# Chunks 2 to 5 of a Mamba-2 scan done as units of 64 tokens, in a fused scan and feed-forward kernel

## The chip, the cores and the metric

One core of a Trainium2 chip runs the whole program. Its engines work in parallel and meet through semaphores: TensorE (matmuls; PE in the profile, with its weight loads as PEld), VectorE (DVE), ScalarE (ACT), GpSimd (POOL) and SyncE (SP), which here issues nearly all DMAs. The metric is the device time of the program in microseconds; less is better.

## The reference

Two layers, one after the other, all in float32. The first is a state-space scan over 4 sequences of 768 tokens with 8 heads, head size 32 and state size 16, cut into chunks. In one chunk, with `cum` the running sum of log `a`:

```python
L = np.exp(cum[:, :, :, None] - cum[:, :, None, :]) * causal
M = np.einsum('bhin,bhjn->bhij', Cc, Bc) * L
y_intra = np.einsum('bhij,bhjd->bhid', M, xc)
y_inter = np.einsum('bhin,bhnd->bhid', Cc, state) * np.exp(cum)[:, :, :, None]
y[:, :, sl] = y_intra + y_inter
Bx = np.einsum('bhjn,bhjd->bhjnd', Bc, xc) * np.exp(cum[:, :, -1:] - cum)[:, :, :, None, None]
state = np.exp(np.sum(la, axis=-1))[:, :, None, None] * state + np.sum(Bx, axis=2)
```

The result doesn't depend on the length of a chunk, only the split of the work between `y_intra` and `y_inter` does. The second layer takes the 3072 rows of 256 values (8 heads of 32):

```python
h = x @ w_in            # 256 -> 2048
g = h * np.cos(h)
out = g @ w_out         # 2048 -> 256
```

## The kernel before

The kernel splits each sequence into 6 chunks (`NC`) of 128 tokens. For each chunk, all 4 sequences give 512 rows for the second layer, which is done in 16 visits (`NF`), 96 in all. A visit `n` with `c, f = divmod(n, 16)` takes half of the rows of chunk `c` and 256 of the 2048 columns: `first(n)` multiplies by `w_in` (line 726), `wind` and `gate` form the cosine (ACT lines 733 and 748, DVE line 739), `gated` multiplies (DVE line 753), `differ` forms three differences on POOL (lines 778 to 781) and `second(n - 2)`, for chunk 1 onward `seven` (line 835), multiplies by `w_out` two visits later (`LAG`). `seven` multiplies 128-column pieces in seven products.

Each engine runs its instructions in the order of the code; there is no scheduler that reorders. Tiles come from pools: a name (tag) has a number of buffers, and the first instruction that writes a new tile waits until the last user of the tile that had the buffer is done. This holds for DMAs too: SP then stands at the DMA, and those behind it in its queue stand as well. The results of `first` have two buffers in PSUM (tag `h`), the products of the scan two pairs of banks (`pair`).

The scan is done between the visits, a chunk ahead of them. Chunks 0 and 1 are done as four units `k` = 0 to 3 of 64 tokens (`W`): `decays0` scans the decays of 64 tokens for all 8 heads and 4 sequences, with the two sequence pairs on the two halves of the partitions; `inner` (line 481) forms C·B, `weights` (DVE line 490) multiplies it with the decays, and `finish0` adds to one result the part of the old state (line 506), the sums for the new state (line 515) and the part of the unit's own tokens (line 523). `weigh0` (POOL line 406) scales B for the sums, in the buffer `sc0`. The times at which units 2 and 3 do this are in `unit_at`: unit 3's `finish0` is at the end of visit 21. `add` in it forms the state after unit 3 on POOL in visit 22, and four DMAs (line 558) move half of it to the partitions where chunk 2 looks for it.

Chunks 2 to 5 are done as 128 tokens of two pairs of sequences `u`. Per chunk: `decays` (line 583, 8 scans), `weigh` (line 566), `reaches` (line 574), `turn_blocks` (transposes on DVE, line 597, of blocks of B and C that `load_blocks` fetched), `turn2` (ACT line 607), `intra2` (line 624), `masked` (line 645, which multiplies only the blocks on and under the diagonal), and after visit 14 of the chunk before, `open2` (lines 656 and 664), `finish2` (line 676) and `carry` (lines 698 and 702), which forms the new state. `plan`, `halves_of` and `block_loads` say in which visits; DVE work that is not a visit's own stands in the list `behind`, one item of it ahead of `gated` and the rest after it.

In the printout that follows, the line numbers are the profile's.

Of the kernel before, what the change touches and what calls it, by code (L numbers as in the profile page):

```python
# [25 lines left out]
def kernel(  # L26
# [31 lines left out]
    rows = ctx.enter_context(tc.tile_pool(name="rows", bufs=NB))  # L58
    scan = ctx.enter_context(tc.tile_pool(name="scan", bufs=2))
    states = ctx.enter_context(tc.tile_pool(name="states", bufs=3))  # L60
# [16 lines left out]
    raw, arow, along, blocks = {}, {}, {}, {}  # L77
# [15 lines left out]
    def load(c, seqs=(0, NB), only=(B, C, x)):  # L93

        if not 1 < c < NC:
            return
        if c not in raw:
            raw[c] = (loads.tile([P, 2, NB * H, N], FP32, tag="bc", name="bc"),
                      loads.tile([P, NB, H, D], FP32, tag="xr", name="xr"))
        bc, xr = raw[c]  # L100
        xr = xr.rearrange("p b h d -> p (b h) d")
        for dst, src in ((bc[:, 0], B), (xr, x)):

            if not any(src is o for o in only):
                continue
            for b in range(*seqs):
                rs = slice(b * H, (b + 1) * H)
                for t in range(2 if b % 2 else 1):
                    n = W if b % 2 else P
                    ts = slice((n - t * W) % P, (n - t * W) % P + n)  # L110
                    nc.sync.dma_start(
                        out=dst[ts, rs], in_=src[b:b + 1, :, c * P + t * W:c * P + t * W + n, :]
                        .rearrange("b h s n -> s (b h) n"))

# [4 lines left out]
    bs, cs = ([t[:, i].rearrange("p (k q h) n -> p k q (h n)", k=2, q=2)[:, k]  # L119
               for t in both for k in range(2)] for i in range(2))  # L120
# [3 lines left out]
    def load_b(k, s, eng=nc.sync, of=B):  # L124

        eng.dma_start(out=(bs if of is B else cs)[k][s * W:(s + 1) * W].rearrange(
# [18 lines left out]
    def group(q, b):  # L145
        return slice(32 * (q ^ b % 2), 32 * (q ^ b % 2) + 32)

    def load_blocks(c, u):
# [3 lines left out]

        blocks[c, u] = to_ = loads.tile([P, 2, 2, 2, 4 * N], FP32, tag="blocks", name="blocks")
        for s in range(2):
            for k, src in enumerate((B, C)):
                of = src[2 * u + s, :, c * P:(c + 1) * P].rearrange(
                    "(q h) (t m) n -> h q t (m n)", h=2, m=4)
                if s == 0:
                    for h in range(2):
# [1021 lines left out]
```

## Time and profile before

| | |
|---|---|
| median of 3 runs | 369.29 us (369.17 to 369.72) |
| the profiled execution | 369.34 us, its span 367.5 us |
| mean granted TensorE clock | 0.998 |
| TensorE busy | 361.1 us (98%) |
| DVE, POOL, ACT busy | 275.3, 217.8, 172.9 us |
| `first` (line 726) | 768 instructions, 183.3 us busy |
| `seven` (line 835) | 1106 instructions, 174.9 us busy in four groups |
| scan matmuls of chunks 2 to 5 (lines 624, 656, 664, 676) | 256, 128, 96, 256 instructions |
| DMA | 30.57 MB, 97706 packets |

A float32 matmul of the code is two instructions in the profile. Small matmuls run beside each other in parts of the array, so their mean durations overlap and don't add up: what a group takes is read from its start to the start of the group behind it, in the timeline. The first line of a group in the timeline holds the start, the time to the end of its last instruction, the engine, the source line, the tiles (output<-inputs), the shape and the number of instructions.

### The profile page before, as it was taken

To read this page: it belongs to the slowest core of one execution; us is meant where nothing else is said; L and a number is where in the kernel's file an instruction comes from. 1 tells how busy PE (TensorE), PEld (TensorE's weight loads), DVE (VectorE), ACT (ScalarE), POOL (GpSimd) and SP (SyncE) were. 2 spreads that over 40 slices of the span, in tenths; PEclk is the share of its full clock that TensorE was granted. 3 is DMA by queue.
4 is the path that set the end of the run, shared out by engine and by line. 5 is a ranking of instruction groups with operands and counts; after the bars stand their busy time and mean duration, and the time that the engine had idled before them with its cause. 6 is when DMAs were issued, how large, how long until landed. Compare 5 with 4: busy or idle time off the path is not lost.

```text
span 367.5 us, 8762 instructions
## 1 busy us (share of the span) xinstructions
PE 361.1 (98%) x3390; PEld 324.9 (88%) x3390; DVE 275.3 (75%) x452; ACT 172.9 (47%) x300; POOL 217.8 (59%) x340
## 2 busy tenths in 40 slices
PE   7999999999999999999999999999999999999995
PEld 4788888899999899999899999989999989999995
DVE  7789998568699857888867987777887783544463
ACT  4588766453445244444344344434444534443432
POOL 6567666679786568765346674544584444554441
PEclk9999999999999999999999999999999999999999
DMA  7996947366226646731054341020100010010011
GB/s 138 264 365 134 213 108 117 47 172 177 62 74 92 137 110 93 219 86 28 18 78 103 97 128 43 0 54 2 28 14 2 0 30 2 2 29 2 0 30 30
DMA packets 97706, 30.57 MB, mean 83 GB/s; under 512 B 71456, under 2 KB 93568, under 8 KB 97664
## 3 DMA queue, kind: packets, MB, share of 16 engines
q1 hardware_dynamic: 96416, 29.61, 35.3%
q8 instruction: 27, 0.44, 0.5%
q10 hardware_dynamic: 1248, 0.39, 0.5%
q14 instruction: 15, 0.12, 0.1%
HBM read 26.58 MB, written 3.34 MB: 81 GB/s over the span
## 4 chain that ended last, share of the span: by engine, by line
PE 91%; DVE 3%; ACT 2%; issue 1%; DMA 1%; SPq 0%; ACTq 0%; DVEq 0%
PE hp L726 44%; PE o L835 34%; PE o L797 6%; PE y L676 2%; PE g L624 2%; DMA bc<-in_B_dram 1%; DVE mag L281 1%; DVE mag L283 1%; PE g L481 1%; PE y L656 1%; PE y L506 1%; PE y L523 1%; DVE w L739 1%; PE o L880 1%; ACT mag L268 0%
## 5 line engine op out<-in xcount | busy, mean ns | idle before, releaser
L726 PE MATMUL hp<-yT,w_in 128*128 128x256 f32 x768 | 183.3, 382 | 0.5 <-DVE gT L753 0.3
L726 PEld LDWEIGHTS hp<-yT,w_in 128*128 128x128 f32 x768 | 139.4, 190 | 19.9 <-issue 3.2
L778 POOL TENSOR_TENSOR gd<-gT 128x256 f32<-128x256 f32 x79 | 60.0, 760 | 97.0 <-DVE gT L753 84.9
L748 ACT ACTIVATE w<-w,quarter 128x512 f32<-128x512 f32 x96 | 69.2, 721 | 83.8 <-DVE w L739 83.7
L739 DVE SCALAR_TENSOR_TENSOR w<-hp,k 128x512 f32<-128x512 f32 x96 | 65.7, 685 | 44.1 <-ACT k L733 43.9
L733 ACT ACTIVATE k<-hp 128x512 int32<-128x512 f32 x96 | 57.0, 594 | 79.7 <-PE hp L726 79.2
L753 DVE TENSOR_TENSOR gT<-hp,w 128x512 f32<-128x512 f32 x96 | 65.3, 680 | 33.2 <-ACT w L748 21.7
L835 PE MATMUL o<-words,gd 128*128 128x128 f32 x474 | 65.9, 275 | 0.0
L835 PEld LDWEIGHTS o<-words,gd 128*128 128x128 f32 x474 | 59.3, 192 | 0.0
L835 PEld LDWEIGHTS o<-w_out,gT 128*128 128x128 f32 x316 | 47.5, 191 | 4.0
L781 POOL TENSOR_TENSOR gd<-gT,gd 128x128 f32<-128x128 f32 x79 | 45.9, 582 | 6.2
L835 PE MATMUL o<-w_out,gT 128*128 128x128 f32 x316 | 48.0, 274 | 0.0
L780 POOL TENSOR_TENSOR gd<-gT,gd 128x128 f32<-128x128 f32 x79 | 44.0, 557 | 6.2
L583 DVE TENSOR_TENSOR_SCAN lam<-arow,unit 128x512 f32<-128x512 f32 x32 | 42.1, 1314 | 0.0
L835 PE MATMUL o<-words,gT 128*128 128x128 f32 x158 | 30.5, 275 | 0.0
L835 PE MATMUL o<-w_out,gd 128*128 128x128 f32 x158 | 30.5, 275 | 0.0
L797 PE MATMUL o<-w_out,gT 128*128 128x256 f32 x128 | 29.9, 379 | 0.0
L797 PEld LDWEIGHTS o<-w_out,gT 128*128 128x128 f32 x128 | 24.2, 190 | 3.3
L645 DVE TENSOR_TENSOR m<-g,lam 128x256 f32<-128x256 f32 x64 | 24.7, 414 | 0.4
L835 PEld LDWEIGHTS o<-words,gT 128*128 128x128 f32 x158 | 24.0, 192 | 0.0
L835 PEld LDWEIGHTS o<-w_out,gd 128*128 128x128 f32 x158 | 24.0, 192 | 0.0
L852 DVE TENSOR_TENSOR sum<-ps,sum 128x256 f32<-128x256 f32 (+1 forms) x27 | 16.6, 639 | 0.6
(113 smaller groups left out, 280.1 us busy)
## 6 DMA issues: line engine op xcount, KB each, us to landing
arow<-a_cut SPq DMA_DIRECT2D x16, 512.0 KB
words<-in_moe_w_in_dram SPq DMA_DIRECT2D x8, 512.0 KB
words<-in_moe_w_out_dram SPq DMA_DIRECT2D x8, 512.0 KB
out_dram<-sum SPq DMA_DIRECT2D x18, 128.0 KB
xr<-in_x_dram SPq DMA_DIRECT2D x16, 128.0 KB
bc<-in_B_dram SPq DMA_DIRECT2D x16, 64.0 KB
xr<-in_x_dram SPq DMA_DIRECT2D x16, 64.0 KB
arow<-a_cut SPq DMA_DIRECT2D x2, 256.0 KB
```

What stands on the lines that cost most here:

```text
L583: V.tensor_tensor_scan(out=lam[c, b][:, hs].rearrange("p h i -> p (h i)"), data0=rows_.rearrange("p h i -> p (h i)"), data1=unit[:, b % 2 ...
L645: V.tensor_tensor(out=m_[js, :, :, is_], in0=g_[js, :, :, is_], in1=l_[js, :, :, is_], op=ALU.mult)
L726: PE.matmul(to_[:, e], lhsT=w_in[:, k, fs], rhs=y[:, k], start=(k == 0), stop=(k == KT - 1), skip_group_check=True)
L733: ACT.activation(k, hp[n], AF.Copy, bias=0.25, scale=INV_2PI)
L739: V.scalar_tensor_tensor(out=w, in0=hp[n], scalar=INV_2PI, in1=k, op0=ALU.mult, op1=ALU.subtract)
L748: ACT.activation(cos, cos, AF.Sin, bias=quarter, scale=TWO_PI)
L753: V.tensor_tensor(out=gT[n], in0=hp.pop(n), in1=cos, op=ALU.mult)
L778: G.tensor_tensor(out=d[:, 0:2], in0=g[:, 1:2].to_broadcast([P, 2, P]), in1=g[:, 3::-3], op=ALU.subtract)
L780: G.tensor_tensor(out=d[:, 2], in0=g[:, 0], in1=d[:, 0], op=ALU.subtract)
L781: G.tensor_tensor(out=d[:, 3], in0=g[:, 2], in1=d[:, 2], op=ALU.subtract)
L797: PE.matmul(o[c, u][:, t], lhsT=g[:, 2 * e + t], rhs=w_out[:, 2 * j + e], start=(j == e == t == 0), stop=(j == NJ - 1 and e == 1), skip_gr ...
L835: PE.matmul(at[q], lhsT=a_[q], rhs=w[q], start=(j == 0 and q in starts), stop=(j == NJ - 1), skip_group_check=True)
```

## The change

Chunks 2 to 5 are done as two units of 64 tokens each, 2c and 2c + 1, as chunks 0 and 1 are; the two units of a chunk share the visits of the second layer (a visit takes one unit of all four sequences where it took a pair of sequences of the whole chunk), the transposes (`turn_blocks`, `turn2`) and the loads. `intra2` and `masked` become `inner2` and `weights`; `decays` and `weigh` become `decays0` and `weigh0`. The sums of a unit's states are formed one chunk ahead: `finish0(3)` also forms those of units 4 and 5, and `open2(c)` those of chunk c + 1; `take_sums` (ACT) copies them out and `add_state` (DVE) adds the decayed state before. `open2` stays behind visit 14, `finish2` moves behind `first` of visit 15, in front of that visit's `wind`. `steps` says in which visits of the chunk before each part is done; loads of chunk 3 start in other visits than before. Left out below are what is removed with the 128-token form (`load_a`, `decays`, `weigh`, `intra2`, `masked`, `carry`, `plan`, `pairs`, `ends`, the wide `unit`), more buffers (2 for `turned` and `cT2`, 2 for `state`), the layouts of `load_b` and of the output's rows, and the loads of chunk 2, whose rows now come in visits 12 and 13, x in 14 and `along` in 15 and 16.

```diff
-    rows = ctx.enter_context(tc.tile_pool(name="rows", bufs=NB))
+    rows = ctx.enter_context(tc.tile_pool(name="rows", bufs=3))
...
+    def load(c):
+        if c < NC:
+            for k in (2 * c, 2 * c + 1):
+                for s in range(2):
+                    load_b(k, s)
+            for k in (2 * c, 2 * c + 1):
+                for s in range(2):
+                    load_x(k, s)
...
+            blocks[c, s] = to_ = loads.tile([P, 2, 2, 2, 4 * N], FP32, tag="blocks", name="blocks")
+            for p in range(2):
+                for k, src in enumerate((B, C)):
...
+                    if s == 0:
+                        for h in range(2):
+                            nc.sync.dma_start(out=to_[:, k, h, p], in_=of[h])
                         yield
...
+                    for q in range(4 if s else 0):
+                        nc.sync.dma_start(out=to_[group(q, s), k, :, p],
+                                          in_=of[:, q].rearrange("h t f -> t h f"))
+                        if q % 2:
+                            yield
...
         for b in seqs:
-            for q in range(4 if b % 2 else 1):
...
+            s = b // 2
+            for q in range(4 if s else 1):
...
     def weigh0(k):
-        scs[k] = sc = scan.tile([P, 2 * H, N], FP32, tag="sc0", bufs=1, name="sc0")
+        scs[k] = sc = scan.tile([P, 2 * H, N], FP32, tag="sc0", bufs=2, name="sc0")
...
+    def sums(k, at, strip, start=False):
...
+        for p in range(2):
+            for s in range(2):
+                ss = slice(s * W, (s + 1) * W)
+                for q in range(4):
+                    r = strip(q, s)
+                    PE.matmul(at[s][r, p * W:(p + 1) * W], lhsT=sc[ss, p, q], rhs=x2[ss, p, q],
+                              start=(start and p == 0), stop=True,
+                              tile_position=(s * W, r.start), skip_group_check=True)
+    def take_sums(c, at):
+        t_ = states.tile([P, 2, 2, 2, 2 * D], FP32, tag="state", name="state")
...
+        for s in range(2):
+            for t in range(2):
+                ts = slice(t * D, (t + 1) * D)
+                ACT.activation(t_[:, 0:len(ks), s, :, ts], at[s][:, 0:len(ks) * P].rearrange(
...
+    def add_state(k):
+        for s in range(2):
+            for p in range(2):
+                i = k % 2 * W + W - 1
+                V.scalar_tensor_tensor(out=after[k][:, s, p], in0=after[k - 1][:, s, p],
+                                       scalar=reach[k // 2, s][:, p, i:i + 1],
+                                       in1=after[k][:, s, p], op0=ALU.mult, op1=ALU.add)
     def finish0(k):
...
+        sums(k, [y[0][:, s, 3 * P:] for s in range(2)], lambda q, s: slice(32 * q, 32 * q + 32),
+             start=(k == 0))
+        if k == 3:
+            at = [y[1][:, s, 2 * P:] for s in range(2)]
+            for i in range(2):
+                sums(4 + i, [ap[:, i * P:(i + 1) * P] for ap in at], group)
...
             for q in range(4):
-                nc.sync.dma_start(out=whole[group(q, 1), :, 1], in_=new[group(q, 0), :, 1])
...
+                nc.sync.dma_start(out=whole[group(q, 1), 1], in_=new[group(q, 0), 1])
+            after[3] = whole
...
+        for k in range(2):
+            i = slice(k * W, (k + 1) * W)
+            V.tensor_tensor_scan(out=reach[c, s][:, p, i], data0=along[c][:, b, i],
+                                 data1=ones[:, 0:W], initial=1.0, op0=ALU.mult, op1=ALU.mult)
...
+    def inner2(c):
         g = [pair("g") for _ in range(2)]
...
+        for k, p, s, q in ((k, p, s, q) for k in range(2) for p in range(2) for s in range(2)
+                           for q in range(4)):
+            bT, cT, _ = part[c, s]
+            r, i = group(q, s), slice(k * W, (k + 1) * W)
+            PE.matmul(g[q // 2][s * W:(s + 1) * W, q % 2, (2 * k + p) * P:(2 * k + p + 1) * P]
+                      .rearrange("p (t i) -> p t i", t=2),
+                      lhsT=bT[r, p, i], rhs=cT[r, p, :, i], start=True, stop=True,
+                      tile_position=(r.start, s * W), skip_group_check=True)
...
     def open2(c):
...
+            r, o_, i = group(q, s), W * (q % 2), (2 * k + p) * W
+            PE.matmul(y[s][o_:o_ + W, q // 2, i:i + W], lhsT=after[2 * c + k - 1][r, s, p],
+                      rhs=part[c, s][2][r, p, k * W:(k + 1) * W], start=(k == p == 0), stop=False,
+                      tile_position=(r.start, o_), skip_group_check=True)
+        for k in range(2 if c < NC - 2 else 1 if c < NC - 1 else 0):
+            sums(2 * c + 2 + k, [y[s][:, 0, (2 + k) * P:(3 + k) * P] for s in range(2)], group)
+    def finish2(c):
+        y = ys.pop(c)
+        for k, p, t, s, q in ((k, p, t, s, q) for k in range(2) for p in range(2)
+                              for t in range(2) for s in range(2) for q in range(4)):
+            ss, i, h = slice(s * W, (s + 1) * W), (2 * k + p) * W, 4 * t + q
+            PE.matmul(y[s][32 * q:32 * q + 32, t, i:i + W], lhsT=xrs[2 * c + k][ss, p, h],
+                      rhs=m_of[2 * c + k][ss, p, h], start=False, stop=True,
+                      tile_position=(s * W, 32 * q), skip_group_check=True)
+        yT[c] = two.tile([P, 2, 2, 2 * P], FP32, tag="yT", name="yT")
+        def take(k):
             for s in range(2):
...
+                ACT.copy(out=yT[c][:, k, :, s * P:(s + 1) * P], in_=y[s][:, :, k * P:(k + 1) * P])
+            if k and c < NC - 1:
+                take_sums(c + 1, [y[s][:, 0, 2 * P:] for s in range(2)])
+        return take
...
+    steps = {c: dict(reach=(5, 6), turn=(6, 7), inner=8, weigh=(9, 10), state=(9, 14),
+                     decays=(8, 10, 11, 13)) if c == 2 else
+             dict(reach=(0, 1), turn=(3, 4), inner=5, weigh=(6, 7), state=(5, 13),
+                  decays=(8, 9, 11, 12)) for c in range(2, NC)}
+    first_decays = (NF + 1, NF + 2, NF + 3, NF + 4)
...
+    def decays2(k, p):
+        decays0(k, p)
+        if p == 1:
+            if k + 2 < 2 * NC:
+                load_arow(k + 2)
+            if k != 2 * NC - 1:
+                weigh0(k)
+    def reaches2(c, s):
+        for b in (2 * s, 2 * s + 1):
+            reaches(c, b)
+            load_along(c + 1, (b,))
+    block_loads = {9 if c == 2 else NF * (c - 2) + 4: c for c in range(2, NC)}
...
-            if c > 0 and f == (NJ if c == 1 else 0):
...
+            if c > 0 and f == (6 if c == 1 else 0):
                 load(c + 2)
...
             first(n)
+            closing = f == NF - 1 and 1 <= c < NC - 1
+            take_y = finish2(c + 1) if closing else None
             wind(n)
...
+            if closing:
+                take_y(0)
+            for e, s in chunks_at(n - 1, "turn"):
+                turn2(e, s)
...
+            behind = [lambda at=at: decays2(*at) for at in decays_at(n)]
+            behind += [lambda c=c, i=i: add_state(2 * c + i) for c, i in chunks_at(n, "state")
+                       if 2 * c + i < 2 * NC - 1]
+            behind += [lambda at=at: reaches2(*at) for at in chunks_at(n, "reach")]
+            behind += [lambda at=at: turn_blocks(*at) for at in chunks_at(n, "turn")]
...
+            behind = [lambda k=2 * c + i, q=q: weights(k, q) for c, i in chunks_at(n, "weigh")
+                      for q in range(2)] + behind
...
             gated(n)
+            if closing:
+                take_y(1)
...
-        for c, u in pairs(n - 1):
...
+        for e, _ in chunks_at(n, "inner"):
+            inner2(e)
...
+        if f == NF - 2 and 1 <= c < NC - 1:
+            open2(c + 1)
+        for at, e in block_loads.items():
             if at == n:
...
+                loading = load_blocks(e)
+            if at <= n < at + 12:
                 next(loading)
```

## The prediction

> **What bounds the kernel now.** I read the page first: engine shares, then the chain.
>
> ```profile
> span 367.5 us, 8762 instructions
> PE 361.1 (98%) x3390; PEld 324.9 (88%) x3390; DVE 275.3 (75%) x452; ACT 172.9 (47%) x300; POOL 217.8 (59%) x340
> ...
> PE 91%; DVE 3%; ACT 2%; issue 1%; DMA 1%; SPq 0%; ACTq 0%; DVEq 0%
> ```
>
> TensorE is busy 98% of the span and 91% of the chain. So work taken off DVE, POOL or the DMA queues is worth nothing by itself: only TensorE's own instructions, or something that makes TensorE wait, can move the end. Next, the stretch from one chunk's `finish2` to the next:
>
> ```profile
> 186.77:244.62 57.85, 57.85 (x552) 53.35 (x548) 46.21 (x78) 25.18 (x43) 33.00 (x55) 1.00 0.33 74
> ```
>
> TensorE is busy for all of 57.85 us, at full clock. Sixteen visits of 1.73 (`first`) + 1.56 (`seven`) us, the pieces in the chain, make 52.64; the other 5.21 are the scan's small matmuls. The timeline of TensorE shows those, of chunk 3 (lines 624 to 676), and of unit 3 (lines 481 to 523), whose shapes the change uses for every unit:
>
> ```profile
> 163.69 0.91 PE L624 MATMUL g<-cT,turned 32*64 32x256 f32 x32
> 164.53 1.99 PE L726 MATMUL hp<-yT,w_in 128*128 128x256 f32 x8
> ...
> 185.49 0.69 PE L656 MATMUL y<-rT,state 32*64 32x128 f32 x32
> 186.12 0.65 PE L664 MATMUL y<-xr,sc 128*32 128x64 f32 x32
> 186.59 1.93 PE L676 MATMUL y<-m,xr 128*32 128x128 f32 x64
> 188.45 1.99 PE L726 MATMUL hp<-yT,w_in 128*128 128x256 f32 x8
> ```
>
> ```profile
> 86.05 0.72 PE L481 MATMUL g<-cT,turned 32*64 32x128 f32 x32
> 86.70 1.99 PE L726 MATMUL hp<-yT,w_in 128*128 128x256 f32 x8
> ...
> 93.47 0.69 PE L506 MATMUL y<-rT,state 32*64 32x64 f32 x32
> 94.10 0.45 PE L515 MATMUL y<-xr,sc 64*32 64x64 f32 x32
> 94.36 0.91 PE L523 MATMUL y<-m,xr 64*32 64x64 f32 x64
> 95.20 1.99 PE L726 MATMUL hp<-yT,w_in 128*128 128x256 f32 x8
> ```
>
> Groups overlap, so I price from start to next start; the profile counts each fp32 matmul of the code as two. Before: L624 0.84 (twice a chunk), L656 0.63, L664 0.47, L676 1.86. The unit's shapes: L481 0.65, L506 0.63, L515 0.26 (8 ns each), L523 0.84. Last, SP's queue and one DVE wait, for the price of a DMA:
>
> ```profile
> 47.09 2.67 SPq L195 DMA_DIRECT2D m<-a_all  x4
> ...
> 103.67 2.64 SPq L558 DMA_DIRECT2D state<-state  x4
> 106.36 3.24 SPq L208 DMA_DIRECT2D along<-a_all  x5
> 109.70 1.21 SPq L160 DMA_DIRECT2D blocks<-in_B_dram  x2
> ```
>
> ```profile
> 51.56 0.78 DVE L455 TENSOR_TENSOR_SCAN m<-m 128x260 f32<-128x260 f32 x1 [0.53 <-DMA m<-a_all]
> ```
>
> ```profile
> SPq L173 <- DVE lam L583: 21.8, 6, 6.9
> ```
>
> A small DMA holds SP 0.60 to 0.66 us. The last of the four at line 195 was issued at 49.76 and DVE, which waited for it, started at 51.56: 1.8 us to landing. The last line shows that a DMA whose destination buffer isn't free stops SP, up to 6.9 us, and all DMAs behind it.
>
> **The change, part by part** (all against the profiled execution: 369.34 us, span 367.5, so 1.84 outside; the median of the runs is 369.29, 0.05 less).
>
> **A, the matmuls.** `intra2` (64 instructions a chunk) becomes `inner2` (64, half the columns); `open2` goes from 32 at 128 columns to 64 at 64; the sums from 32 a chunk (three chunks) to 32 a unit (seven units); `finish2` from 64 to 128 at half size. Removed: 4 x (2 x 0.84 + 0.63 + 1.86) + 3 x 0.47 = 18.1 us. Added, by doubling each unit row: 4 x (1.30 + 1.26 + 1.68) + 7 x 0.26 = 18.8. But those rows hold a drain at a change of shape that doubling shouldn't repeat: read finer, the timeline has L481 and L506 start 32 instructions within 0.45, L523 its 64 within 0.70. Second halves at those rates: 4 x (1.10 + 1.08 + 1.54) + 1.8 = 16.7, so -1.4. If `open2` and `finish2` reach L515's 8 ns plus 0.2 of drain: 4 x (1.10 + 0.72 + 1.24) + 1.8 = 14.0, so -4.1. I take -1.4, since L523 is `finish2`'s exact shape; ends -4.1 and +0.7. Insertions between visits stay at three a chunk (the two `intra2`, and `open2` with `finish2`; now `inner2`, `open2`, `finish2`), so their edges, (5.21 - 4.64) / 3 = 0.19 each, cancel.
>
> The Trainium skill, "TensorE: Matmul & The Clock Gate", section "Wait — 56ns, not 53.3ns?", speaks against this part: starts of matmuls never come closer than about 25 ns, however small. By it the 1248 added instructions would take an estimated 31.2 us, 13.1 more than what they replace. L515's 32 starts in 0.26 us contradict it for tiles side by side, and I go by the row.
>
> **B, `sc0`.** Two buffers, three tiles alive: unit 3's is read in `finish0(3)` (end of visit 21), units 4's and 5's are written in visits 18 and 20. So `weigh0(5)` on POOL must wait for unit 3's sums, while `finish0(3)` now also runs the sums of units 4 and 5. TensorE then waits: 0.64 (L406) + about 0.3 of hand-over both ways, less 0.26 for unit 4's sums: +0.7, with a late start about +0.8; ends 0 and 1.2. Queued behind `weigh0(5)` on POOL is `differ(20)` (0.76 + 0.56 + 0.58), wanted by `seven(20)` a `first` later, after 1.83 us: just in time.
>
> **C, SP's queue and the state of unit 3.** This decides. The load of blocks of chunk 3 starts in visit 20 (before: 23). Its tag has two buffers, so its first DMA waits for `turn_blocks(2, 0)`, which DVE does in visit 22. SP stands, and behind that DMA are queued, in code order: the second of the pair, two `along` and two block DMAs (visit 21), `load(3)` with 8 (now in visit 22, was 24), 8 `along` of `reaches2(2, 1)`, and only then the four that put half of unit 3's state, `whole`, in its place. Before, those four went out as POOL finished (103.67), and were needed 27 us later; now `add_state(4)` on DVE reads `whole` in visit 25.
>
> Times from the end of `first(22)`, called T (97.03 before, about 98.2 after A and B). The transposes end at T + 5.5 (102.49 before, by DVE's timeline; ACT's extra copies of `take_sums` in visit 21, 4 x 0.36, delay this by up to 1, and I take none). 22 DMAs at 0.60 to 0.66: 14.2; the four: 2.6; landing 1.8: T + 24.1. DVE gets to `add_state(4)` about T + 15 and stands. Queued behind it are `wind_w(26)` and all of visit 26; ACT waits for `wind_w`, POOL for `gated`. TensorE goes on until `first(28)` wants the buffer of `hp[26]`: T + 11.2 (end of `first(25)`, with `inner2`) + 1.56 x 3 + 1.73 x 2 = T + 19.3. Released: landing, two products (0.55), `wind_w` 0.69, sine 0.72, `gated` 0.68 and four hand-overs of 0.1 = T + 27.1. TensorE waits 7.8. Then DVE is behind: visits 26 and 27 hold `weights(5, 1)` 0.68 and scans of 1.22, and by the same walk `first(29)` waits 1.1 more: about +9.0. Ends: 0, if the slot wait isn't there (B1 below), and 12, with 0.75 a DMA, a landing of 3.3 (line 945's store to line 195) and a late transpose.
>
> **D, cT.** `turn2(c, 1)` is now in the visit of `inner2`. ACT: 0.1 + 0.59 + two at 0.46 = 1.6 after `first`; `seven` ends at 1.56. +0.1 a chunk, +0.4; ends 0 and 0.8.
>
> **E, the end of a chunk.** `finish2` moves behind `first(15)` of the chunk, and the next `first` needs `take_y(0)`: two copies (0.65 as a pair, L532) and 0.2 of hand-over, hidden by `seven`, 1.56. Slack 0.7; 0 taken, ends 0 and +4 (1 us each). ACT then has `take_y(1)` and four copies of sums (0.65 + 1.45) before `wind_k`, late by 0.8; LAG = 2 leaves 2.3 to `seven`.
>
> **At nothing**, since TensorE doesn't wait for them: DVE loses the 64-row and 128-row products (26.5 us in all), half of the scans and `carry`, and gains `weights`, more short scans and `add_state` (some -30 us net); POOL loses its masks and two copies; the rows' DMAs fall from 512 to 256 KB. Were the cover gone, they would be gains; none of them ends last in the table above.
>
> Sum: -1.4 + 0.8 + 9.0 + 0.4 = +8.8; 369.3 + 8.8 = 378.1.
>
> **Rivals.** *B1, C doesn't bite*: the state lands before T + 16.4, the point from which TensorE waits (19.3 less the 2.9 of the release); SP would have to start its 18.6 us at T - 2.2. For it: SP is idle from 92.7 to 99.8 before, and without the slot wait the 22 DMAs would be out by then or soon after. Against: two tiles of chunk 2 hold both buffers. Time: -1.4 + 0.8 + 0.4 = -0.2: 369.1, from 366.0 (A at -4.1, B and D less) to 371.2. This is the faster side, decided by A below -1.4. *B2, no C but E*: copies late at four boundaries, 1 us each, and A at +0.7: about 374. For it: the path from `finish2` to `first` is now 0.85 long where a whole visit lay between; against: the slack of 0.7. *B3, TensorE doesn't change*: the matmuls equal out (+0.7 - 0.7) and waits are hidden: within B1's range.
>
> **How the numbers follow.** C bites 0.70, with 373.5 to 382 as its own range (A's ends and C's 12); B1 and B3 0.20, of which faster 0.13, same 0.06, slower 0.01; B2 0.10, slower. A measurement here tells 0.2% (0.7 us) from no change. Faster 0.13, same 0.06, slower 0.81. The range 368.3 to 382 leaves out the lower part of B1 (0.1) and a longer C (0.07).
>
> **What would show it.** A: `finish2`'s 128 starts in about 1.5 us, `open2` with sums in 1.6. B: TensorE idle about 0.7 between sums in `finish0(3)`, released by POOL's `sc`. C: SP idle until the transposes, the state's DMAs some 16 us after them, DVE idle before the first `add_state` with a DMA named, and TensorE idle 7 to 9 us near 118 to 127 us, the only long gap; chunks 3 to 5 at about 57.3 us. E: no idle TensorE before a chunk's first `first`. Wrong if: the state's DMAs leave before 105 us, or small matmuls start slower than 13 ns.

## The result, and the profile after

The changed kernel takes 381.43 us (median of four runs, 380.64 to 382.51), the kernel before 369.38 (369.17 to 369.72, four runs): a ratio of 1.0327, with a 95% interval of 1.0301 to 1.0354. It is slower by 3.3%, 3.3 us more than the 378.1 predicted and inside the range. The profiled execution took 381.46 us with a span of 379.6, so 12.1 us more of span.

The page of the changed kernel, shares first, then the slices of TensorE and its granted clock, then the chain:

```profile
span 379.6 us, 9750 instructions
PE 363.1 (96%) x3902; PEld 326.3 (86%) x3902; DVE 250.3 (66%) x420; ACT 177.8 (47%) x324; POOL 202.8 (53%) x327
...
PE   8999999999896599999999999999999999999996
...
PEclk9999999999999699999999999999999999999999
...
PE 83%; POOL 5%; DVE 4%; SPq 3%; issue 2%; ACT 2%; DMA 0%; POOLq 0%; DVEq 0%; ACTq 0%
```

DVE lost 25.0 us of work, POOL 15.0, and the DMAs went from 30.57 to 26.39 MB; TensorE is busy 2.0 us longer, and its share fell from 98% to 96%. The digits that fell most, 6 and 5, are slices 13 and 14 (114 to 133 us), and the granted clock has its only 6 in the second of them. To see where the 12.1 us are, I took the starts of `first(n)` in the timeline of TensorE, after less before:

| from the start of | to | change, us | what is in it |
|---|---|---|---|
| the span | `first(16)` | -0.35 | |
| `first(16)` | `first(22)` | +3.70 | unit 3's `finish0`, with the sums of units 4 and 5 |
| `first(22)` | `first(25)` | +0.30 | |
| `first(25)` | `first(28)` | +7.59 | the wait for the state |
| `first(28)` | `first(32)` | +2.02 | slow clock; `open2`, `finish2` of chunk 2 |
| `first(32)` | `first(48)` | +0.74 | small matmuls of chunk 3 |
| `first(48)` | `first(64)` | -1.05 | small matmuls of chunk 4 |
| `first(64)` | `first(80)` | -0.71 | small matmuls of chunk 5 |
| `first(80)` | the end | -0.14 | |

**The state.** Four groups of the table of waits (engine, line, what it waited for; total us, times, longest):

```profile
DVE state L503 <- DMA state<-state: 8.7, 1, 8.7
PE hp L667 <- DVE gT L694: 7.8, 2, 7.4
PE y L637 <- issue: 1.6, 2, 0.9
PE y L481 <- POOL sc L385: 1.4, 1, 1.4
```

The queue of SP, where each line is a group of DMAs from its first issue to its last:

```profile
98.44 2.14 SPq L154 DMA_DIRECT2D blocks<-in_C_dram  x2
104.62 1.27 SPq L151 DMA_DIRECT2D blocks<-in_B_dram  x2
...
120.72 2.50 SPq L571 DMA_DIRECT2D state<-state  x4
```

And DVE:

```profile
103.45 1.14 DVE L590 STREAM_TRANSPOSE turned<-blocks 128x256 f32<-128x256 f32 x2
...
124.54 0.48 DVE L503 SCALAR_TENSOR_TENSOR state<-state,reach,state 128x64 f32<-128x64 f32 x2 [8.68 <-DMA state<-state]
```

SP stands from 100.6 until the transposes of DVE are done (103.45 + 1.14), and then works off its queue. The state's four DMAs go out from 120.72; DVE, which has waited 8.68 us at `add_state(4)`, goes on at 124.54. TensorE in the same stretch:

```profile
95.09 0.86 PE L481 MATMUL y<-xr,sc 64*32 64x64 f32 x64
...
97.37 0.46 PE L481 MATMUL y<-xr,sc 64*32 64x64 f32 x32 [1.42 <-POOL sc L385]
97.63 0.98 PE L534 MATMUL y<-m,xr 64*32 64x64 f32 x64
...
127.31 3.75 PE L667 MATMUL hp<-yT,w_in 128*128 128x256 f32 x8 [7.43 <-DVE gT L694]
130.86 0.97 PE L775 MATMUL o<-w_out,gT 128*128 128x128 f32 x4
...
132.78 1.89 PE L667 MATMUL hp<-yT,w_in 128*128 128x256 f32 x8
```

The wait before `first(28)`, at 127.31, is 7.43 us. What follows it is slow: `first(28)` takes 3.55 us to the next start where a `first` takes 1.73 to 1.83, and `seven(26)` 1.92 in place of 1.56. The answer for windows has the reason (length, busy time of each engine, then the granted clock, DMA share and GB/s):

```profile
119.80:127.30 7.50, 0.08 (x1) 0.02 (x1) 2.50 (x6) 1.21 (x2) 0.00 (x0) 0.83 0.14 35
127.30:128.50 1.20, 1.19 (x3) 1.02 (x4) 1.20 (x2) 0.00 (x0) 1.11 (x2) 0.50 0.19 41
130.90:132.80 1.90, 1.90 (x16) 1.90 (x15) 1.36 (x3) 0.88 (x2) 1.53 (x3) 0.81 0.85 130
132.80:135.00 2.20, 2.20 (x15) 1.99 (x14) 1.63 (x3) 0.67 (x2) 1.41 (x3) 1.00 0.00 0
```

After 7.4 us without work TensorE had a clock of 0.50, and the full one again only in the fourth window (the trace's record of the clock has 0.50 from 124.78 to 131.61). Of the 7.59 + 2.02 us, 7.43 are the wait and (3.55 - 1.83) + (1.92 - 1.56) = 2.1 the clock. The rest is chunk 2's small matmuls, with a stop that comes up below.

**Unit 3.** In the TensorE lines above, the sums of units 3 and 4 (64 instructions at 95.09) end at 95.95, and those of unit 5 start at 97.37: 1.42 us for POOL's `sc`. The timeline of POOL:

```profile
86.46 1.56 POOL L385 TENSOR_TENSOR sc<-bc,lam 128x256 f32<-128x256 f32 x1
...
91.79 1.32 POOL L721 TENSOR_TENSOR gd<-gT,gd 128x128 f32<-128x128 f32 x1
...
93.60 1.27 POOL L713 TENSOR_TENSOR words<-w_out,words 128x512 f32<-128x512 f32 x1
...
96.67 0.64 POOL L385 TENSOR_TENSOR sc<-bc,lam 128x256 f32<-128x256 f32 x1
```

`weigh0(5)`, at 96.67, comes late. Whether a buffer or the work ahead of it holds it is a question for an experiment.

**The small matmuls of chunks 2 to 5.** The timeline of TensorE at the end of three chunks' scans:

```profile
143.01 0.34 PE L637 MATMUL y<-m,xr 64*32 64x64 f32 x16
144.22 1.44 PE L637 MATMUL y<-m,xr 64*32 64x64 f32 x112 [0.86 <-issue]
...
201.81 1.28 PE L637 MATMUL y<-m,xr 64*32 64x64 f32 x105
203.82 0.42 PE L637 MATMUL y<-m,xr 64*32 64x64 f32 x23 [0.73 <-issue]
...
256.70 0.91 PE L625 MATMUL y<-rT,state 32*64 32x64 f32 x64
257.54 0.46 PE L481 MATMUL y<-xr,sc 64*32 64x64 f32 x32
257.93 1.99 PE L667 MATMUL hp<-yT,w_in 128*128 128x256 f32 x8
259.85 1.48 PE L637 MATMUL y<-m,xr 64*32 64x64 f32 x128
```

In chunk 4 (the last four lines) `open2` takes 0.84, the sums of one unit 0.39, `finish2` 1.41, each to the start of the group behind it. In chunks 2 and 3 `finish2` stops in the middle, after 16 and after 105 of its 128 instructions, for 0.86 and 0.73 us, and the profile names no semaphore ("issue").

**What the stops are.** The page's list of DMA queues has a queue by the name of instruction. First of the kernel before, then of the kernel after (packets, MB, share):

```profile
q8 instruction: 27, 0.44, 0.5%
```

```profile
q8 instruction: 31, 0.51, 0.6%
```

That is 16 KB a packet, and 27 became 31. TensorE has 3390 matmuls, as many weight loads and 124 other instructions in the trace before, 6904 in all, and 3902, 3902 and 107 in the trace after, 7911: 1007 more, 3.9 times 256. That made me take these packets for TensorE's own program, 256 instructions each. It can be held against the trace, which has the time of each packet. I numbered TensorE's instructions in their order, laid a grid over them (a border after the first 449 instructions, which have no packet here, and then after each 256; the same for every kernel of this study), and gave each border its packet, in order. No view gives the 449: what speaks for it is that this one value fits all kernels. At the two stops of the changed kernel:

```
                  border before   packet starts   landed   TensorE goes on
chunk 2                  139.68          141.89   142.77            144.22
chunk 3                  199.59          201.55   202.54            203.82
```

At both, TensorE goes on 1.45 and 1.28 us after the block has landed. In the eleven kernels with the new scan (this one and the ten below) the timelines show 34 stops of 0.19 us or more as "issue"; all lie within 4 instructions of a border of this grid, and at all of them TensorE goes on 1.19 to 1.67 us after the packet landed. Over all borders of the twelve kernels no block was in use earlier than 1.19 us after its landing. So a stop with "issue" is TensorE waiting for its next block. A block starts on its way at about the time when the one ahead of it is begun (2.2 and 2.0 us later in the two rows), so borders that come close together leave it little time: the shortest distance in the kernel before is 3.97 us, after the change 2.63, 3.15 and 3.20. These are in the stretch from `open2` to `finish2`, which now has 512 instructions in small matmuls and weight loads (256 before) and one `first` between them. But closeness alone makes no stop. At these three shortest distances there is none, since the packet started 0.2 to 0.7 us after the border before it. At the two stops TensorE came to the border later, 3.7 and 3.5 us after the one before, and stopped because the packet had started 2.2 and 2.0 us after that one.

### The profile page after: what moved, and what is told of

Its sections match the earlier page's. It is cut to its first block, busy times and chain, and to the rows that moved or that the text cites. A ratio compares the mean times of both kernels' runs of the same rounds, so it can differ in the third digit from the quotient of the medians.

```text
span 379.6 us, 9750 instructions
## 1 busy us (share of the span) xinstructions
PE 363.1 (96%) x3902; PEld 326.3 (86%) x3902; DVE 250.3 (66%) x420; ACT 177.8 (47%) x324; POOL 202.8 (53%) x327
## 2 busy tenths in 40 slices
DMA packets 97324, 26.39 MB, mean 70 GB/s; under 512 B 87328, under 2 KB 93184, under 8 KB 97280
## 4 chain that ended last, share of the span: by engine, by line
PE 83%; POOL 5%; DVE 4%; SPq 3%; issue 2%; ACT 2%; DMA 0%; POOLq 0%; DVEq 0%; ACTq 0%
PE hp L667 39%; PE o L775 30%; PE o L737 5%; PE y L637 2%; POOL words L713 1%; SPq L192 1%; PE g L611 1%; POOL gd L719 1%; POOL gd L721 1%; DVE mag L265 1%; PE y L625 1%; DVE mag L267 1%; DVE w L680 1%; PE y L481 1%; SPq L123 1%
## 5 line engine op out<-in xcount | busy, mean ns | idle before, releaser
L719 POOL TENSOR_TENSOR gd<-gT 128x256 f32<-128x256 f32 x79 | 59.0, 746 | 129.8 <-DVE gT L694 125.6
L775 PE MATMUL o<-w_out,gT 128*128 128x128 f32 x316 | 48.8, 277 | 0.0
L721 POOL TENSOR_TENSOR gd<-gT,gd 128x128 f32<-128x128 f32 x79 | 41.2, 522 | 6.2
L722 POOL TENSOR_TENSOR gd<-gT,gd 128x128 f32<-128x128 f32 x79 | 38.7, 490 | 6.2
L379 DVE TENSOR_TENSOR_SCAN lam<-arow,unit 128x512 f32<-128x512 f32 x20 | 28.9, 1444 | 0.0
L737 PEld LDWEIGHTS o<-w_out,gT 128*128 128x128 f32 x128 | 24.2, 190 | 3.3
L469 DVE TENSOR_TENSOR m<-g,lam 128x512 f32<-128x512 f32 x24 | 16.1, 679 | 0.5 <-PE g L460 0.5
```

What stands on the lines that cost most here:

```text
L379: V.tensor_tensor_scan(out=lams[k][:, p, hs].rearrange(flat), data0=rows_.rearrange(flat), data1=unit0[:, hs].rearrange(flat), initial=0.0 ...
L719: G.tensor_tensor(out=d[:, 0:2], in0=g[:, 1:2].to_broadcast([P, 2, P]), in1=g[:, 3::-3], op=ALU.subtract)
L721: G.tensor_tensor(out=d[:, 2], in0=g[:, 0], in1=d[:, 0], op=ALU.subtract)
L722: G.tensor_tensor(out=d[:, 3], in0=g[:, 2], in1=d[:, 2], op=ALU.subtract)
L737: PE.matmul(o[c, u][:, t], lhsT=g[:, 2 * e + t], rhs=w_out[:, 2 * j + e], start=(j == e == t == 0), stop=(j == NJ - 1 and e == 1), skip_gr ...
L775: PE.matmul(at[q], lhsT=a_[q], rhs=w[q], start=(j == 0 and q in starts), stop=(j == NJ - 1), skip_group_check=True)
```

## The experiments

Times are medians; the kernel before was run again beside each group, at 369.95 us (the first four), 369.77 (`e5` to `e8`) and 370.03 (the last two).

**1. Chunk 3's blocks later.** The load of chunk 3's blocks starts in visit 23, as before the change, when the transposes are done. The load of rows, the loads behind it and all work of DVE stay.

```diff
-    block_loads = {9 if c == 2 else NF * (c - 2) + 4: c for c in range(2, NC)}
+    block_loads = {9 if c == 2 else NF + 7 if c == 3 else NF * (c - 2) + 4: c
+                   for c in range(2, NC)}
```

> Only the load of chunk 3's blocks moves from visit 20 to visit 23, behind the transposes that free its buffer, so that SP doesn't stand. Theory of the queue: SP, free at about 100.6 us, works off the 18 DMAs that are left ahead of the state's four (18 x 0.63 = 11.4, 2.5 for the four, 1.8 to landing), the state is there at about 116 to 118 us and not at 124.5; TensorE's wait of 7.4 before first(28) falls to 0 to 1.2, and the slow clock behind it (about 2.1) goes: 371.9 to 373.1 us. Rival, DVE is overloaded in visits 25 to 27 with products, scans and add_state and the DMA is not what counts: nothing changes, 381 us.

374.67 us, a ratio of 1.0133 (1.0109 to 1.0157). From its timelines of SP, DVE and TensorE:

```profile
114.66 2.50 SPq L571 DMA_DIRECT2D state<-state  x4
```

```profile
118.49 0.48 DVE L503 SCALAR_TENSOR_TENSOR state<-state,reach,state 128x64 f32<-128x64 f32 x2 [1.87 <-DMA state<-state]
```

```profile
121.27 1.97 PE L667 MATMUL hp<-yT,w_in 128*128 128x256 f32 x8 [0.63 <-DVE gT L694]
```

SP no longer stands, the state goes out 6.06 us earlier, and the wait of TensorE falls from 7.43 to 0.63 us, with 0.87 more one visit later. The slow clock is gone with it: that `first` takes 1.97 us to its end, not 3.75. The time misses the expectation by 1.6: 6.8 us came back of the 8.0 that these lines would give (7.43 + 2.1 - 0.63 - 0.87). This profiled execution has stops for instructions of 0.4, 0.87 and 0.21 us. It also has a wait that the changed kernel does not have, in `inner2` of chunk 3:

```profile
160.74 1.14 PE L611 MATMUL g<-cT,turned 32*64 32x128 f32 x56 [1.26 <-ACT cT L599]
```

The blocks of chunk 3, begun three visits later, were not all there when DVE wanted to transpose them (it waited 2.31 us for a DMA, until 159.11), so the move has a price of its own.

**2. The load of chunk 3's rows later.** Eight of the 22 DMAs ahead of the state go two visits later; SP still stands at the buffer.

```diff
-            if c > 0 and f == (6 if c == 1 else 0):
+            if c > 0 and f == (8 if c == 1 else 0):
```

> Only load(3) moves back from visit 22 to visit 24, so that 8 of the 22 DMAs stand behind the state's four; SP still stands for the buffer until 104.6 us. Theory of the queue: 14 DMAs x 0.63 = 8.8 and 2.5 and 1.8 make the state land at about 117.7 us, 6.9 earlier; TensorE's wait falls from 7.4 to about 0.6 and the slow clock goes: 372.5 us. Rival, DVE overloaded: 381 us. Rival, the wait for the buffer alone is what counts, and the number of DMAs behind it isn't: also near 381.

375.64 us, 1.0143 (1.0113 to 1.0174). DVE, then TensorE:

```profile
117.26 0.48 DVE L503 SCALAR_TENSOR_TENSOR state<-state,reach,state 128x64 f32<-128x64 f32 x2 [1.48 <-DMA state<-state]
```

```profile
120.04 1.97 PE L667 MATMUL hp<-yT,w_in 128*128 128x256 f32 x8 [0.24 <-DVE gT L694]
...
141.58 2.57 PE L667 MATMUL hp<-yT,w_in 128*128 128x256 f32 x6 [2.78 <-issue]
```

The eight DMAs were worth what their issue times say: the state's went out at 113.44 and not 120.72. Together with the first experiment, the wait for the state is settled as the queue of SP: it is 22 DMAs long and starts with one whose buffer is taken. A DVE with too much work is refuted as the cause, since in both its work is as it was. `first(29)` waits 0.87 us here too. The time missed by 3.1: the last line has a stop of 2.78 us at a border (its packet started 3.45 us after the border before it and landed 1.51 us ahead of the restart), and the clock was 0.50 for 3.41 us behind it. The profiled execution took 377.10, so not all of this is in the median.

**3. The first state later.** `add_state(4)` in visit 29, in place of 25, so that nothing is waiting when the state comes late.

```diff
-    steps = {c: dict(reach=(5, 6), turn=(6, 7), inner=8, weigh=(9, 10), state=(9, 14),
+    steps = {c: dict(reach=(5, 6), turn=(6, 7), inner=8, weigh=(9, 10), state=(13, 14),
```

> Only add_state(4) moves from visit 25 to visit 29 (state=(13, 14)); SP's queue is left as it is. Theory of the queue: the state still lands at about 124.5 us, DVE asks for it after about 123 us at the earliest and stands little or not; TensorE's wait of 7.4 and the slow clock of 2.1 go: 371.9 us. Rival, the four visits' place doesn't matter because a wait of the same length comes up later: 376 to 381 us. This run alone doesn't tell the queue from an overloaded DVE; with the two that leave DVE's work where it is it does.

374.32 us, 1.0124 (1.0105 to 1.0143). DVE has no wait for the state, and no `first` of these visits waits. SP's queue is as long as it was (the state's DMAs at 121.80), and costs nothing: C is a matter of who waits. The expectation of 371.9 is missed by 2.4. TensorE's timeline has stops of 1.83, 0.80 and 0.20 us, the first two of them:

```profile
136.53 1.39 PE L637 MATMUL y<-m,xr 64*32 64x64 f32 x111 [1.83 <-issue]
...
196.05 0.42 PE L637 MATMUL y<-m,xr 64*32 64x64 f32 x23 [0.80 <-issue]
```

The places are those of the changed kernel, the lengths are not.

**4. A third buffer for `sc0`.** If `weigh0(5)` waits for the buffer of unit 3, as step B had it, a third buffer ends that.

```diff
-        scs[k] = sc = scan.tile([P, 2 * H, N], FP32, tag="sc0", bufs=2, name="sc0")
+        scs[k] = sc = scan.tile([P, 2 * H, N], FP32, tag="sc0", bufs=3, name="sc0")
```

> Only sc0 gets three buffers, so that weigh0(5) on POOL needn't wait for unit 3's sums. Theory: TensorE's wait of 1.4 inside finish0(3) goes, and C, whose times hang on visit 22, stays as long as it is: 380.0 us; POOL's weigh0(5) then falls into visit 20 and may hold differ(20) by up to 0.6. Rival, the wait in finish0(3) is for POOL being busy at all (it has the differences of w_out to do there) and not for the buffer: no change, 381.4.

383.08 us, 1.0347 (1.0306 to 1.0389), and TensorE's wait is what it was:

```profile
98.67 0.46 PE L481 MATMUL y<-xr,sc 64*32 64x64 f32 x32 [1.42 <-POOL sc L385]
```

The buffer isn't the cause. POOL's queue had the same order as in the changed kernel. The expected 380.0 is missed; the interval overlaps that of the changed kernel.

**5. `weigh0` of units 4 and 5 on DVE.** On top of experiment 3. It takes 2.2 us of work (1.56 + 0.64) out of POOL's queue.

```diff
-        G.tensor_tensor(out=sc, in0=bs[k].rearrange("p q (h n) -> p (q h) n", h=H),
+        eng = V if k in (4, 5) else G
+        eng.tensor_tensor(out=sc, in0=bs[k].rearrange("p q (h n) -> p (q h) n", h=H),
```

> add_state(4) in visit 29 as in e3_state_later (374.3 us, TensorE's wait inside finish0(3) 1.41), and weigh0 of units 4 and 5 on DVE instead of POOL. Theory: the 1.41 come from POOL's backlog of differences in visits 16 to 20, not from the buffer of sc0, so the wait goes wholly, and POOL is relieved of 1.56 and 0.64 us ahead of the differences that seven(18) and seven(19) want: 372.0 to 372.9. Rival, DVE is no earlier (its scan of unit 5 ends in the same visit): 374.

371.86 us (six runs), 1.0054 (1.0034 to 1.0073).

```profile
96.42 0.46 PE L482 MATMUL y<-xr,sc 64*32 64x64 f32 x32 [0.30 <-DVE sc L386]
...
133.75 1.44 PE L638 MATMUL y<-m,xr 64*32 64x64 f32 x111 [0.68 <-issue]
...
194.25 0.42 PE L638 MATMUL y<-m,xr 64*32 64x64 f32 x22 [1.16 <-issue]
```

The wait of 1.42 becomes 0.30, and 2.5 us are gained over experiment 3: POOL's queue was the cause in B. This is the best form of the new scan in this study, and still 0.5% slower than the kernel before. The stops in its timeline add up to 0.4 + 0.68 + 0.2 + 1.16 + 0.2 = 2.6 us; the profiled execution was 3.0 over the median of the kernel before.

**6. `finish2` in two halves.** On top of experiment 3: the products of the second unit move behind `seven` of the same visit, so that `seven` lies between two groups of 64.

```diff
+        def multiply(k):
+            for p, t, s, q in ((p, t, s, q) for p in range(2)
+                               for t in range(2) for s in range(2) for q in range(4)):
...
+        multiply(0)
...
-        return take
+        return take, lambda: multiply(1)
...
-            if closing:
-                take_y(1)
...
+        if n < NC * NF and closing:
+            multiply_y()
+            take_y(1)
```

> As e3_state_later, and finish2's second unit moves behind seven of the same visit, so that the 256 TensorE instructions of finish2 (weights and products) no longer come in one burst. Theory, the gaps in finish2 in front of which the profile names only issue (1.8, 0.8 and 0.2 us in e3, at the 16th, 105th and 122nd of 128 products in every kernel) are TensorE waiting for its next block of instructions, used up too fast: the gaps of chunks 3 and 5 go (-1.0), that of chunk 2 stays, since what comes before it is unchanged, and four more edges of 0.19 cost +0.8: 374.1. Rival, they are waits inside finish2 for banks or copies: the split changes their places and they stay as long, 375 to 377 with the copies now later.

374.00 us, 1.0109 (1.0086 to 1.0131): as expected, and the same as experiment 3. In the `finish2` of chunks 3 and 5 there is no stop any more (0.2 us are left at a border ahead of chunk 3's); in chunk 2 it stays, and the next border has one too:

```profile
135.85 0.71 PE L639 MATMUL y<-m,xr 64*32 64x64 f32 x47 [1.13 <-issue]
...
140.51 1.46 PE L670 MATMUL hp<-yT,w_in 128*128 128x256 f32 x6 [0.77 <-issue]
```

**7. Loads out of the way.** On top of experiment 3: the loads of rows start in the fifth visit of a chunk, not in the first, so that the data is not on its way when `finish2` runs.

```diff
-            if c > 0 and f == (6 if c == 1 else 0):
+            if c > 0 and f == (6 if c == 1 else 4):
```

> As e3_state_later, and the loads of chunks 4 and 5 start in visit 4 of chunks 2 and 3 instead of visit 0, away from finish2. Theory, the instruction blocks come through the same DMA engines as the data and are late when these are full (share 0.44 to 0.84 ahead of the long gaps, 0 ahead of the gap of 0.2): the gap of chunk 3 falls from 0.8 to 0.2 or less, that of chunk 2, with the backlog of SP still in front of it, from 1.8 to between 0.2 and 1.0: 372.3 to 373.5. Rival, data DMAs have no part in it: 374.3.

374.99 us, 1.0122 (1.0091 to 1.0153), over a wide spread: no gain that can be told, where 372.3 to 373.5 was expected. In chunk 3 the stop went from 0.80 to 0.46 us, in chunk 2 from 1.83 to 0.71, but at the next border, in a `first` at 141.08, there is one of 1.41. The packets of instructions say more than the time. In the `finish2` of chunk 3, over the eleven kernels, the packet started 0.8 to 1.5 us after the border before it where the DMA engines were busy up to 0.18 in between, and 1.7 to 2.2 us after it where they were busy 0.37 to 0.51. At the second border of chunk 2 there is no such order (1.07 us at a share of 0.96, 3.45 at 0.88). That transfers of data delay the blocks is suggested by the one and not by the other, and stays open.

**8. All three**: 5, 6 and 7 together.

> All three together on top of e3_state_later: weigh0 of units 4 and 5 on DVE, finish2 split, loads away from finish2. Theory: -1.9 for the first, -1.0 to -1.8 for the others: 370.5 to 371.5, still not under the kernel before (369.4 to 370.0), because the smaller matmuls save only 0.7 to 1.0 a chunk and the sums that units 4 and 5 add in finish0(3) cost 0.5 to 0.9. Rival, without waits the new form is the faster one: 368.

372.43 us, 1.0071 (1.0059 to 1.0084), against 370.5 to 371.5 expected: not better than experiment 5 alone. Its stops are 0.94 us in chunk 2 and 0.83 at the border behind, with packets that started 2.7 and 2.5 us after the border ahead of theirs. It is 1.7 us over the median of the kernel before in its profiled execution, and these stops are 1.8.

**9 and 10. Other places for the borders.** Experiment 5 with small matmuls at the start whose product nobody reads, 16 of them, or 40 (32 and 80 instructions of TensorE, with as many weight loads). They move the borders by 64 and 160 instructions. The rest of the work is unchanged.

```diff
+    more = bank([P, 4, P], "warm", "o")
+    for _ in range(16):
+        PE.matmul(more[:, 0, 0:8], lhsT=nc.const_aps.tensor(1.0, (P, P), FP32),
+                  rhs=nc.const_aps.tensor(1.0, (P, 8), FP32), start=True, stop=True,
+                  skip_group_check=True)
```

> As e5_weigh_on_dve, with 16 tiny matmuls more at the very start of TensorE's program (their results aren't used), while it waits for the first loads anyway. Theory, the gaps of finish2 are the borders of blocks of 256 TensorE instructions: 16 matmuls are 64 instructions, as many as 32 of finish2's products, so every gap moves 32 products earlier: in chunk 3 from the 106th of 128 to the 74th, in chunk 5 from the 123rd to the 91st, in chunk 2 from the 17th out of finish2 into the sums ahead of it, with a new border at about the 113th. Rival, the gaps hang on something in finish2 itself (banks, the copies, the state): they stay at 17, 106 and 123. Time by either: 371 to 374, since the borders only move.

> As e9_pad_16 with 40 tiny matmuls, 160 instructions, 80 products: gaps, by the theory of the blocks, at about the 26th product of chunk 3, the 43rd of chunk 5 and the 65th of chunk 2; by the rival at 17, 106 and 123. Time by either: 371 to 374.

384.68 us (1.0395, 1.0352 to 1.0437) and 389.97 (1.0542, 1.0499 to 1.0584). The times are missed by far and tell nothing of the stops in question: the added matmuls took 4.0 and 16.9 us at the start, and with 16 of them borders fell into the start and brought stops of 2.89 and 2.18 us, each with 3.41 us of half clock behind it. The places are what these two were run for. With 16, TensorE's timeline has

```profile
148.30 0.34 PE L638 MATMUL y<-m,xr 64*32 64x64 f32 x15 [1.21 <-issue]
...
204.57 0.99 PE L638 MATMUL y<-m,xr 64*32 64x64 f32 x74
206.16 0.78 PE L638 MATMUL y<-m,xr 64*32 64x64 f32 x54 [0.60 <-issue]
```

The stop of chunk 2 went from after the 17th matmul to after the 113th (17 - 32, and one block of 128 pairs on), that of chunk 3 from the 106th to the 74th, as blocks of 256 want it and as no cause in the work itself would. With 40 the borders fell after the 65th and the 26th, and `finish2` has no stop: the two blocks landed 11.0 and 1.35 us ahead. In chunk 5, where experiment 5 stops for 0.2 us, neither has one. The chunks 3, 4 and 5 of the kernel with 40 take -0.35, -1.13 and -0.78 us against the kernel before, which is what the new matmuls are worth when TensorE has its instructions.

## Why the prediction was right, and where not

Against the sum of the prediction, in us of the span:

| step | predicted | measured |
|---|---|---|
| A, small matmuls | -1.4 | -0.1: -1.7, and 1.6 of stops for instructions |
| B, `sc0` | +0.8 | +2.0: a wait of 1.4, and 0.6 at `seven(19)`, which waits for POOL too |
| C, SP's queue | +9.0 | +9.5: 7.4 of waiting and 2.1 of slow clock |
| D and E | +0.4 | 0 |
| in no step | | +0.7 |
| sum | +8.8 | +12.1 |

A is worked out from the intervals of the first table: 0.30 + 7.59 + 2.02 - 7.43 - 2.08 = 0.40 for chunk 2, then 0.74, -1.05 and -0.71, and 0.53 for the sums of units 4 and 5 in `finish0(3)` (0.79 for two units less 0.26 for one before). The 0.7 in no step are 0.78 up to `first(21)`, 0.4 more around those sums, and -0.5 at the start and the end.

**C was right in its mechanism, and its size was in part luck.** The state's DMAs stand in SP's queue behind 22 others that a taken buffer holds; T, the end of `first(22)`, was 100.38, DVE went on with the state at T + 24.2 (predicted T + 24.1), and the wait was 7.43 us (predicted 7.8). Experiments 1, 2 and 3 take it away in three ways and leave 0.63, 0.24 and 0. The close times hide errors that cancel: SP went on at T + 4.2 and not T + 5.5, the 22 DMAs took 16.1 us and not 14.2, and from the state's first DMA to DVE it was 3.8 and not 4.4. The 1.1 us that the walk gave `first(29)` are 0.87 in experiments 1 and 2; in the changed kernel they did not show, since TensorE itself was late: the clock was at half speed after the idle time, 2.1 us, a term that the prediction did not have. So the 9.0 predicted and the 9.5 measured are not the same sum. The Trainium skill, "TensorE: Matmul & The Clock Gate", "Part 1: The HAM clock gate", has such a drop after an idle window of about 3.4 us. The runs agree with the window as a unit: 0.50 held for 6.83 us here and for 3.41 in experiments 2, 9 and 10. They disagree on the idle time that it takes: in experiment 2 a stop of 2.78 us was enough, in experiment 10 one of 1.82. Which stops were enough is in the last section.

**B failed in its cause.** "`weigh0(5)` on POOL must wait for unit 3's sums" is refuted by experiment 4: with a third buffer the same 1.42. What holds it is POOL's order: `weigh0(4)` takes 1.56 us at 86.46 and `differ` and `differ_w` are queued behind it, so that POOL, without a pause between them, gets to `weigh0(5)` at 96.67; the sums whose buffer it was to wait for had ended at 95.95. Experiment 5, which takes the two off POOL, leaves 0.30 and takes 2.5 us off the time. The prediction looked at what is queued behind `weigh0(5)` and not at what is queued ahead of it, and a price taken from a buffer's release (0.64 and some hand-over) could not see a queue.

**A was right in its rows, and missed a term.** The starts came as the unit's rows gave them: `inner2` 1.14 (1.10 predicted), `open2` 0.84 (1.08), the sums of one unit 0.39 and of two 0.79 (0.26 and 0.52), `finish2` 1.41 (1.54). That is 4.18 with two units' sums, against 4.24 predicted and 4.64 before: a small gain, as predicted. The missing term is the supply of instructions: 512 matmuls more are 27 to 31 blocks, and between `open2` and `finish2` they are at times used up faster than they come. It is 1.6 us in the changed kernel and 1.5 to 3.7 in experiments 1 to 8. It is also most of what parts the rival B1, 369.1 without C, from experiment 5, which has neither C nor B and takes 371.9, with stops of 2.6 us. Experiment 3, without C alone, has 374.3.

The Trainium skill's rule that was weighed (the same page, "Wait — 56ns, not 53.3ns?"), starts never closer than about 25 ns, doesn't hold for the new shapes either, whose matmuls lie side by side in the array: chunk 4's `finish2` has its 128 instructions done in 1.48 us, 11.6 ns each. The 13.1 us that it gave come near the result, by a cause that isn't there.

**D and E**: apart from 0.5 us for `cT` at the very start, which the kernel before has too, no wait for `cT` and none at a chunk's first `first` shows in the table of waits. The 25 us less on DVE and 15 on POOL were worth nothing, as the prediction said of them (it had some 30 on DVE).

**The rivals.** B1 and B3, without C, were ruled out by the wait; B2 by E at 0. As a case, C (70%) came in, within its own range of 373.5 to 382, near the upper end.

## What to carry to other kernels

When a step is moved, list everything that its queue does ahead of it and look for the one entry whose buffer is not free: its delay falls on all that stand behind, and only the one that somebody waits for costs time, so that either the entry or the one who waits can be moved. Before small matmuls are traded for fewer columns, count the instructions and not only their starts: a stop with "issue" and no semaphore, at places that repeat with a fixed number of instructions, was TensorE waiting for its program here. And an engine's mean share is no cover (POOL was busy for 53% of the span, and TensorE waited 1.42 us for it): look at the visits where the new instruction runs.

## What the hardware showed that I had not expected

- TensorE's program comes in packets of 16 KB, 256 instructions with the weight loads counted. Packets took 0.88 to 1.73 us, and a block was never in use earlier than 1.19 us after its packet had landed; where TensorE came to a border within 4.2 us of the one before, it stopped or not by that distance and by when the packet had started; the stops are of 0.2 to 2.9 us in these runs. Why one packet starts 1.0 us after the border before it and another 3.5 is open.
- Stops of 1.82, 2.18, 2.78 and 2.89 us were each followed by 3.41 us at a clock of 0.50, one of 1.83 in experiment 3 was not. The traces' records of the clock show what tells them apart: within each trace all changes of the clock lie on a grid of 3.41 us that runs through, whatever TensorE does. The four stops lay each within one such stretch, that of experiment 3 was divided by a border of the grid (idle is the time without a matmul). The clock fell at the end of the stretch:

```
                stop            stretch         idle in it   clock in the next
experiment 10   113.92-115.74   113.78-117.19      1.82          0.50
experiment 9     18.13- 21.02    18.10- 21.52      2.89          0.50
experiment 9     25.14- 27.31    24.93- 28.34      2.18          0.50
experiment 2    138.80-141.58   138.56-141.98      2.78          0.50
experiment 3    134.70-136.53   132.02-135.43      0.73          1.00
                                135.43-138.84      1.10          1.00
```

  Over the twelve kernels, the most idle time in a stretch that left the clock at 1.00 was 1.58 us (experiment 6, at its end). So in these runs not the length of a stop counts, but how much of one stretch is idle, and the grid lies elsewhere in each trace.
- A matmul with 128 x 128 weights and 8 columns started every 0.21 us where 80 stood in a row at the start, and every 0.11 us for most of the 32. The clock is what differs:

```profile
3.46 4.11 PE L833 MATMUL warm<-const-float32-1.0 128*128 128x8 f32 x32
```

```profile
3.46 17.07 PE L833 MATMUL warm<-const-float32-1.0 128*128 128x8 f32 x80
```

  The trace with 32 (experiment 9) has a clock of 1.00 from 4.45, and there the starts go from 0.21 to 0.11 us apart; the trace with 80 (experiment 10) has it only from 25.03, after them. With 32 the clock fell to 0.50 again at 7.86, behind a stretch in which TensorE had next to nothing but these matmuls, and no stop. So here these small matmuls, one behind the other, neither raised the clock nor held it.
